# Converting every weight on VectorE, in a new place in the order, and a later cast of the gate, in a fused attention and gated-MLP kernel

## The chip, the core and the metric

The kernel runs on one core of one Trainium2 chip. Its time is the device time of one execution in microseconds (us). A core has five engines with a queue of instructions each: TensorE (PE, with its weight loads shown apart as PEld), VectorE (DVE), ScalarE (ACT), GpSimd (POOL) and SyncE (SP), which here issues all transfers between the large memory and the on-chip memories. Matmuls write to PSUM, a small memory that the kernel uses in three buffers of two banks for most products and in two single banks for the attention's sums.

## The reference

Sigmoid attention over 8 batches, 12 heads, 448 positions and a head size of 64, and behind it a gated MLP with a spatial mix over the positions:

```
scores = q @ k.T / sqrt(64) - log(448)
x      = sigmoid(scores) @ v                   # per batch and head; heads side by side: 448 x 768
h      = max(x @ w_in, 0)                      # 448 x 1024
u, v   = h[:, :512], h[:, 512:]
v_n    = (v - mean(v)) / sqrt(var(v) + 1e-6)   # over the 512 columns
v_s    = w_spatial @ v_n + b_spatial[:, None]
out    = (u * v_s) @ w_out                     # 448 x 768
```

All inputs are 32-bit floats, but w_in and w_out reach the core as 64-bit words, two 32-bit halves an element, which the kernel itself brings into 32-bit floats.

## The kernel before, in words

**Split products.** Outside the attention's second product every operand is held as two parts, hi (the value rounded by a copy into the matmul's 32-bit type) and lo (the value less hi). `split` (lines 99 to 101) makes them: a copy by the engine that it is given, then a subtraction on VectorE. A product takes three matmuls, hi·hi, lo·hi, hi·lo (`TERMS`, line 223).

**Order.** `in_program_order` (lines 18 to 32) ties each engine's instructions to the order in which the program issues them. What stands behind a waiting instruction on its engine waits as well. Waits between engines, and which buffer of a pool a tile gets, are worked out by the tile framework. Python generators interleave the parts: each `next` issues the instructions up to the next `yield`.

**Rounds.** The eight batches go in four rounds m of two (b0 and b1). A round is: attention for both batches, `gate_values` for 7 row tiles in groups of 2, 2, 2, 1 (matmuls pv, 126 of them; relu rv on ScalarE, line 309; statistics and normalization on VectorE and POOL, lines 313 to 337), `spatial` for b0 in two pairs (matmuls pg; addition of the bias on VectorE, line 366), `gated` for b0 in two pairs (matmuls pu; the product g on VectorE, line 388; its split gs, cast on ScalarE and subtraction on VectorE), `spatial` for b1, `output` for b0 in three pairs (matmuls po; copy on ScalarE, line 421; transfer out), `gated` for b1, and `output` for b1. pv, pg, pu, po and the attention's score tiles psc all take their turn in the same three PSUM buffers.

**Attention.** `attention(m)` is a generator: it splits q and k of the first pair of heads, yields, computes three score tiles (psc on TensorE, then a sigmoid at on ScalarE, line 256), yields, and then does the rest. In a round that is not the last, the splits of the next round's attention stand behind `gated(b1, pairs[0])`, the first three score tiles behind `gated(b1, pairs[1])`, and `output` for b1 behind them.

**Weights.** `weight_steps` (lines 140 to 183) is a generator over 22 weights: the first 13 (`NFIRST`, line 186) are six of w_in's second half with the four of w_spatial among them and three of w_in's first half; numbers 13 to 15 are the rest of w_in, 16 to 21 the six blocks of w_out. Each weight first issues the load of the weight two further on (line 159). For a weight below 13, `convert` and the split run on VectorE in three steps. From 13 on (`scalar`), a scaling (line 122) and the copy to hi (line 177) are on ScalarE, VectorE does the rest, and there are four steps. All of it belongs to round 0: attention of round 0 issues 33 steps, one behind most score tiles; the rest are issued by `load_weights(YB)` and its like in lines 490 to 500, ahead of each part of round 0. Two of the 33 steps belong to weight 13.

Of the kernel before, what the change touches and what calls it, by code (L numbers as in the profile page):

```python
# [35 lines left out]
def attn_gmlp_kernel(  # L36
# [67 lines left out]
        return ps_2.tile([P, 2, 512], F32, tag="ps2", name=name)  # L104


    YB = 4

    def convert(l, raw, scalar):

        r = raw.rearrange("p (n w) -> p w n", w=2)
        low, a = r[:, 0], r[:, 1]
        nc.vector.tensor_scalar(l, a, 0x80000000, None, op0=ALU.bitwise_and)


        af = a.bitcast(F32)
        bound = 122879.9921875
        if scalar:

            nc.vector.tensor_scalar(af, af, -bound, bound, op0=ALU.max, op1=ALU.min)  # L120
            yield
            nc.scalar.mul(af, af, 2.0**-112)
        else:
            nc.vector.tensor_scalar(
                a, a, 1, 1, op0=ALU.logical_shift_left, op1=ALU.logical_shift_right
            )
            nc.vector.tensor_scalar(af, af, bound, 2.0**-112, op0=ALU.min, op1=ALU.mult)
        yield
        nc.vector.scalar_tensor_tensor(  # L129
            l, a, 3, l, op0=ALU.logical_shift_left, op1=ALU.bitwise_or  # L130
        )
        nc.vector.scalar_tensor_tensor(  # L132
            l, low, 29, l, op0=ALU.logical_shift_right, op1=ALU.bitwise_or
        )
        yield
# [4 lines left out]
    def weight_steps():  # L140

        steps = []
        for i in range(NCC):
            steps += [(w_in, w_in_s, NCC + i)] + [(w_sp, w_sp_s, i)] * (i < NFC)
        steps += [(w_in, w_in_s, i) for i in range(NCC)]
        steps += [(w_out, w_out_s, i) for i in range(NFC * DM // 512)]
        raws = {}

        def load(n):
            if n < len(steps):  # L150
                src, _, i = steps[n]
                w = 512 if src is w_sp else 1024

                if n < NFIRST:
                    raw = work.tile([P, 1024], U32, tag="tmp", name=f"wraw_{n}", bufs=3)[:, :w]
                else:
                    raw = work.tile([P, 1024], U32, tag="raw", name=f"wraw_{n}", bufs=4)
                raws[n] = raw.bitcast(F32) if src is w_sp else raw
                nc.sync.dma_start(raws[n], src[:, i * w : (i + 1) * w])

        for n in range(AHEAD):
            load(n)
        yield
        for n, (src, dst, i) in enumerate(steps):
            load(n + AHEAD)
            if src is w_sp and i == 0:
                nc.sync.dma_start(b_bc, b_sp.broadcast_to([P, 512]))
            hi, lo = dst[:, i, 0], dst[:, i, 1]
            scalar = n >= NFIRST
            val = raws.pop(n)  # L170
            if src is not w_sp:
                raw = val
                val = work.tile([P, 512], U32, tag="wval", name=f"wval_{n}", bufs=1)
                yield from convert(val, raw, scalar)
                val = val.bitcast(F32)
            if scalar:
                nc.scalar.copy(hi, val)
                yield
            else:
                nc.vector.tensor_copy(hi, val)  # L180
            nc.vector.tensor_sub(lo, val, hi.bitcast(F32))
            if not scalar:
                yield


    NFIRST = NCC + NFC + 3

    weights = weight_steps()

    def load_weights(n):  # L190
        for _ in range(n):
            next(weights, None)
# [152 lines left out]
    def spatial(b, fcs):  # L345

        odd = b % 2
        cols = cols_of(b)
        pg = banks(f"pg_{b}_{fcs[0]}")
        for i, fc in enumerate(fcs):  # L350
            fs = slice(fc * P, (fc + 1) * P)
            pairs = []
            for c in range(NFULL):
                vn = vns[c + 4 if odd else c]
                pairs.append(
                    (lambda a, vn=vn: vn[:, a, fs], lambda p, c=c: w_sp_s[:, c, p, cols])
                )

            short = vns[NFULL][:, odd, fs]
            product(  # L360
                pg[:, i, :S], pairs, [(short, w_sp_s[:, NFULL, a, cols]) for a in range(2)]
            )
        g = work.tile([P, 2, 512], F32, tag="tmp", name=f"g_{b}_{fcs[0]}", bufs=3)[:, :, :S]
        bb = b_bc[:, cols]
        bb = bass.AP(bb.tensor, bb.offset, [list(bb.ap[0]), [0, 2], list(bb.ap[1])])
        nc.vector.tensor_add(g, pg[:, :, :S], bb)
        gates[b, fcs] = g

    hidden = {}

    def gated(b, fcs):

        odd = b % 2
        g = gates.pop((b, fcs))
        pu = banks(f"pu_{b}_{fcs[0]}")
        for i, fc in enumerate(fcs):
            fs = slice(fc * P, (fc + 1) * P)
            product(
                pu[:, i, :S],
                [  # L380
                    (
                        lambda a, cc=cc: w_in_s[:, cc, a, fs],
                        lambda c, cc=cc: x_s[:, c, cc, odd * S : (odd + 1) * S],
                    )
                    for cc in range(NCC)
                ],
            )
        nc.vector.scalar_tensor_tensor(g, pu[:, :, :S], 0.0, g, op0=ALU.max, op1=ALU.mult)  # L388
        gs = work.tile([P, 2, 2 * S], F32R, tag="split", name=f"gs_{b}_{fcs[0]}", bufs=3)
        gs = gs.rearrange("p a (i s) -> p a i s", i=2)  # L390
        split(gs[:, 0], gs[:, 1], g, nc.scalar.copy)
        for i, fc in enumerate(fcs):
            hidden[b, fc] = gs[:, :, i]
# [36 lines left out]
    def start_loads(m):  # L430
        n = m * 2 * NHP
        ahead(attention_loads, n)
        ahead(attention_loads, n + 1)
        ahead(value_loads, n)
        ahead(attention_loads, n + 2)

    def attention(m):

        first, end = 2 * NHP * m, 2 * NHP * (m + 1)
        waiting = []  # L440

        def scores(n, tiles):
            for t in tiles:
                if t == 1:
                    ahead(attention_splits, n + 1)
                if n + 2 < end and t == NFULL + 1:
                    ahead(attention_splits, n + 2)
                waiting.append((*units[n], t, attention_scores(*units[n], t)))
                if n + 2 < end:
                    if t == 0:  # L450
                        ahead(attention_loads, n + 3)
                        ahead(value_loads, n + 2)
                    elif t == NFULL and n + 4 < end:
                        ahead(attention_loads, n + 4)
                if m == 0 and (n > first or t > NFULL) and t != 2:
                    load_weights(1)

        def sums(n):
            for args in waiting[:n]:
                attention_values(*args)  # L460
            del waiting[:n]

        attention_splits(*units[first])
        yield
        for n in range(first, end, 2):
            scores(n, range(NFULL))
            if n == first:
                yield
            scores(n, [NFULL])
            sums(NFULL + (n > first))  # L470
            scores(n, range(NFULL + 1, TILES))
            sums(len(waiting) - NFULL - 1)
        sums(NFULL + 1)
# [13 lines left out]
    for m in range(B // 2):  # L487
        for _ in running:
            pass
        load_weights(YB)  # L490
        for ts in ((0, 1), (2, 3), (4, 5), (6,)):
            load_weights(YB)
            gate_values(m, ts)
        b0, b1 = 2 * m, 2 * m + 1
        for fcs in pairs:
            load_weights(YB)
            spatial(b0, fcs)
        for fcs in pairs:
            load_weights(2 * YB)
            gated(b0, fcs)  # L500
        for fcs in pairs:
            spatial(b1, fcs)
        start_loads(m + 1)
        for es in outs:
            output(b0, es)
        gated(b1, pairs[0])
        last = m == B // 2 - 1
        if not last:
            running = attention(m + 1)
            next(running)  # L510
        gated(b1, pairs[1])
        if not last:
            next(running)
        early = outs if last else outs[:1]
        for part in range(2):
            for es in early:
                output(b1, es, part)
        for es in outs[len(early) :]:
            output(b1, es)
# [53 lines left out]
```

## Time and profile before

| what | us |
|---|---|
| median of 3 runs (lowest, highest) | 702.55 (702.3, 702.74) |
| the profiled execution, its own time | 703.04 |
| its span, first to last instruction | 701.3 |
| TensorE busy | 685.6 (98%) |
| VectorE busy | 285.6 (41%) |
| ScalarE busy | 252.2 (36%) |
| mean granted TensorE clock | 0.994 |

A row of a timeline gives the start in us from the span's start, the length, the engine, the line, the operation, the tile written and those read, the shapes and a count; behind it, in brackets, stands how long the engine had been idle and which instruction ended that. A row of waits gives the engine and tile that waited, what released it, and the total in us, the number of times and the longest. A clock of 1.00 is TensorE's full granted speed.

### The profile page before, as it was taken

The page shows a single profiled execution, that of the slowest core. Times are in us where ns is not written, and L with a number is a line of the kernel's source. Part 1 is how long each engine was busy: PE and PEld are TensorE (multiplying, and loading weights), DVE is VectorE, ACT ScalarE, POOL GpSimd, SP SyncE. Part 2 cuts the span into 40 slices and gives each one's busy share as a digit, 9 for nine tenths or more (in the row PEclk, how much of TensorE's full clock was granted, in tenths as well). Part 3 has the DMA queues.
Part 4 walks back from the last instruction along what each step waited for, and adds up shares of the span by engine and source line. Part 5 has one row for each costly group of instructions (what it writes and reads, how often), then busy time and mean ns, then how long its engine had stood idle before and what let it go on. Part 6 is the DMA issues. An engine that isn't in the chain of part 4 may idle for free.

```text
span 701.3 us, 9100 instructions
## 1 busy us (share of the span) xinstructions
PE 685.6 (98%) x3839; PEld 506.4 (72%) x3839; DVE 285.6 (41%) x451; ACT 252.2 (36%) x302; POOL 18.5 (3%) x36
## 2 busy tenths in 40 slices
PE   9999996999999999999999999999999999999997
PEld 5454885998745468999864548899985455889996
DVE  6997767714124326420414233722122341462110
ACT  6887221212286711001347761101135764101111
POOL 0000001000000001000000000100000000110000
PEclk9999998999999999999999999999999999999999
DMA  8872221212344300003044320000305320000102
GB/s 314 292 251 82 60 61 57 79 59 72 106 157 133 106 1 0 1 1 131 1 158 158 117 68 0 1 1 26 106 27 195 101 73 1 1 1 0 53 27 79
DMA packets 20392, 55.37 MB, mean 79 GB/s; under 512 B 1920, under 2 KB 8192, under 8 KB 20352
## 3 DMA queue, kind: packets, MB, share of 16 engines
q1 hardware_dynamic: 20352, 54.80, 23.1%
q8 instruction: 30, 0.49, 0.3%
q14 instruction: 10, 0.08, 0.0%
HBM read 43.78 MB, written 11.01 MB: 78 GB/s over the span
## 4 chain that ended last, share of the span: by engine, by line
PE 91%; DVE 4%; ACT 2%; issue 1%; POOL 1%; DMA 0%; ACTq 0%; SPq 0%
PE pav L278 19%; PE pu L289 17%; PE po L289 17%; PE psc L248 13%; PE pv L289 12%; PE pg L289 9%; PE psc L236 3%; DVE vn L330 1%; DVE stats L313 1%; ACT rv L309 1%; DVE wval L132 1%; PE idle L482 0%; DVE g L388 0%; DVE wval L129 0%; DVE vn L329 0%
## 5 line engine op out<-in xcount | busy, mean ns | idle before, releaser
L256 ACT ACTIVATE at<-psc,bias_s 128x896 f32<-128x896 f32 x168 | 158.2, 1008 | 42.5 <-PE psc L248 40.1
L278 PE MATMUL pav<-at,v 128*64 128x448 f32 (+1 forms) x768 | 139.4, 546 | 0.0
L289 PE MATMUL pu<-x_s,w_in_s 128*128 128x448 f32 x576 | 120.6, 370 | 5.7 <-ACT rv L309 5.7
L289 PE MATMUL po<-gs,w_out_s 128*128 128x448 f32 x576 | 119.9, 368 | 3.0 <-ACT at L256 3.0
L289 PEld LDWEIGHTS pu<-x_s,w_in_s 128*128 128x128 f32 x576 | 110.0, 191 | 15.2 <-ACT rv L309 6.1
L289 PEld LDWEIGHTS po<-gs,w_out_s 128*128 128x128 f32 x576 | 107.9, 188 | 14.1 <-ACT at L256 4.1
L289 PE MATMUL pv<-w_in_s,x_s 128*128 128x512 f32 x504 | 115.4, 390 | 0.0
L289 PEld LDWEIGHTS pv<-w_in_s,x_s 128*128 128x128 f32 x504 | 94.3, 188 | 22.3 <-issue 2.8
L248 PEld LDWEIGHTS psc<-qks 64*128 64x128 f32 x864 | 77.1, 186 | 39.4 <-ACT at L256 15.5
L278 PEld LDWEIGHTS pav<-at,v 128*64 128x64 f32 (+1 forms) x768 | 44.0, 135 | 82.2 <-issue 75.5
L248 PE MATMUL psc<-qks 64*128 64x448 f32 x864 | 103.0, 378 | 0.2
L101 DVE TENSOR_TENSOR x_s<-pav,x_s 128x448 fp32r<-128x448 f32 x48 | 29.6, 623 | 127.3 <-ACT x_s L100 127.3
L289 PE MATMUL pg<-w_sp_s,vn 128*128 128x448 f32 x352 | 73.2, 365 | 0.8 <-ACT rv L309 0.8
L289 PEld LDWEIGHTS pg<-w_sp_s,vn 128*128 128x128 f32 x352 | 65.9, 187 | 7.0 <-ACT rv L309 1.1
L388 DVE SCALAR_TENSOR_TENSOR g<-pu,g 128x896 f32<-128x896 f32 x16 | 17.5, 1091 | 126.0 <-PE pu L289 126.0
L421 ACT COPY osb<-po 128x896 f32<-128x896 f32 x24 | 21.8, 907 | 119.2 <-PE po L289 108.6
L100 ACT CAST gs<-g 128x896 fp32r<-128x896 f32 x16 | 15.1, 942 | 128.8 <-DVE g L388 128.8
L101 DVE TENSOR_TENSOR qks<-raw,qks 128x832 fp32r<-128x832 f32 (+2 forms) x49 | 49.3, 1007 | 4.7 <-ACT qks L100 3.3
L309 ACT ACTIVATE rv<-pv 128x1024 f32<-128x1024 f32 (+1 forms) x16 | 14.6, 914 | 75.7 <-PE pv L289 75.7
L100 DVE CAST qks<-raw 128x832 fp32r<-128x832 f32 (+1 forms) x39 | 22.6, 578 | 38.5 <-PE po L289 36.4
L313 DVE BATCH_NORM_STATS2 stats<-rv 128x6 f32<-128x512 f32 x28 | 19.0, 679 | 42.9 <-ACT rv L309 42.9
L100 ACT CAST x_s<-pav 128x448 fp32r<-128x448 f32 x48 | 25.5, 532 | 27.8 <-PE pav L278 27.8
(36 smaller groups left out, 231.7 us busy)
## 6 DMA issues: line engine op xcount, KB each, us to landing
raw<-qk_dram SPq DMA_DIRECT2D x47, 448.0 KB, 4.3
v<-v_dram SPq DMA_DIRECT2D x24, 448.0 KB, 4.7
out_dram<-osb SPq DMA_DIRECT2D x24, 448.0 KB, 2.6
wraw<-w_in_dram SPq DMA_DIRECT2D x12, 512.0 KB, 4.1
wraw<-w_out_dram SPq DMA_DIRECT2D x6, 512.0 KB, 3.8
wraw<-w_sp_dram SPq DMA_DIRECT2D x4, 256.0 KB, 5.2
raw<-qk_dram SPq DMA_DIRECT2D x1, 320.0 KB, 3.0
b_bc<-b_sp_dram SPq DMA_DIRECT2D x1, 256.0 KB, 5.8
```

Source lines behind the costliest of these rows:

```text
L100: copy(hi, src)
L101: nc.vector.tensor_sub(lo, src, hi.bitcast(F32))
L132: nc.vector.scalar_tensor_tensor(l, low, 29, l, op0=ALU.logical_shift_right, op1=ALU.bitwise_or)
L236: nc.tensor.matmul(psc[odd * HALF : (odd + 1) * HALF, j, :S], raw[rows, PART : PART + HALF], raw[rows, REST:PART], start=True, stop=True,)
L248: nc.tensor.matmul(psc[:, j, :S], s[rows, a, k : k + P], s[rows, e, REST:PART], start=i == 0, stop=i == len(TERMS) - 1,)
L256: nc.scalar.activation(at, psc[:, :, :S], AF.Sigmoid, bias=bias_s, scale=QK)
L278: nc.tensor.matmul(pav[heads, :S], vt[rows, t, heads], at[rows, j], start=start, stop=stop)
L289: nc.tensor.matmul(ps, st, mv, start=start and i == 0, stop=stop and i == len(ops) - 1)
L309: nc.scalar.activation(rv[:, :n], pv[:, :n], AF.Relu)
L313: nc.vector.bn_stats(stats, rv[:, i])
L388: nc.vector.scalar_tensor_tensor(g, pu[:, :, :S], 0.0, g, op0=ALU.max, op1=ALU.mult)
L421: nc.scalar.copy(osb, po[:, :, :S])
```

## The change

It has two parts. First, the form with ScalarE is gone from `convert` and `weight_steps`: every weight is converted in three steps on VectorE alone, with the two instructions (shift, then bound and scale) that stood only below weight 13, and with the copy to hi on VectorE. The calls that issue the steps move too. Behind round 0's attention stand six steps in one go, before the first normalization; then one step behind each group of `gate_values`; then three steps behind each `spatial` and `gated` of b0 and behind each `spatial` of b1. Before, four steps stood ahead of each part, eight ahead of each `gated`, and none at `spatial` of b1.

Second, `gated` is cut in two: `gated` ends with the product, and `gated_splits` issues the cast and the subtraction. Everywhere but at one place the two stand together. For the second pair of b1, in a round that is not the last, the first score tile of the next round (and its sigmoid) is issued between them. For this `attention` yields behind each of its first three score tiles.

```
-    def convert(l, raw, scalar):
+    def convert(l, raw):
...
-        if scalar:
-
-            nc.vector.tensor_scalar(af, af, -bound, bound, op0=ALU.max, op1=ALU.min)
-            yield
-            nc.scalar.mul(af, af, 2.0**-112)
-        else:
-            nc.vector.tensor_scalar(
-                a, a, 1, 1, op0=ALU.logical_shift_left, op1=ALU.logical_shift_right
-            )
-            nc.vector.tensor_scalar(af, af, bound, 2.0**-112, op0=ALU.min, op1=ALU.mult)
+        nc.vector.tensor_scalar(
+            a, a, 1, 1, op0=ALU.logical_shift_left, op1=ALU.logical_shift_right
+        )
+        nc.vector.tensor_scalar(af, af, bound, 2.0**-112, op0=ALU.min, op1=ALU.mult)
         yield
...
-            if scalar:
-                nc.scalar.copy(hi, val)
-                yield
-            else:
-                nc.vector.tensor_copy(hi, val)
-            nc.vector.tensor_sub(lo, val, hi.bitcast(F32))
-            if not scalar:
-                yield
+            split(hi, lo, val, nc.vector.tensor_copy)
+            yield
...
+    BLOCK = 3
...
         nc.vector.scalar_tensor_tensor(g, pu[:, :, :S], 0.0, g, op0=ALU.max, op1=ALU.mult)
+        products[b, fcs] = g
+
+    def gated_splits(b, fcs):
+
+        g = products.pop((b, fcs))
         gs = work.tile([P, 2, 2 * S], F32R, tag="split", name=f"gs_{b}_{fcs[0]}", bufs=3)
...
-            scores(n, range(NFULL))
-            if n == first:
-                yield
+            for t in range(NFULL):
+                scores(n, [t])
+                if n == first:
+                    yield
...
-        load_weights(YB)
+        load_weights(2 * BLOCK)
         for ts in ((0, 1), (2, 3), (4, 5), (6,)):
-            load_weights(YB)
             gate_values(m, ts)
+            load_weights(1)
         b0, b1 = 2 * m, 2 * m + 1
         for fcs in pairs:
-            load_weights(YB)
             spatial(b0, fcs)
+            load_weights(BLOCK)
         for fcs in pairs:
-            load_weights(2 * YB)
             gated(b0, fcs)
+            gated_splits(b0, fcs)
+            load_weights(BLOCK)
         for fcs in pairs:
             spatial(b1, fcs)
+            load_weights(BLOCK)
...
         gated(b1, pairs[0])
+        gated_splits(b1, pairs[0])
...
         gated(b1, pairs[1])
         if not last:
             next(running)
+        gated_splits(b1, pairs[1])
+        if not last:
+            next(running)
+            next(running)
```

More of the change, by code (lines that the diff above doesn't have):

```diff
@@ L104, in banks @@
         return ps_2.tile([P, 2, 512], F32, tag="ps2", name=name)
-    YB = 4
-    def convert(l, raw, scalar):
+    def convert(l, raw):
         r = raw.rearrange("p (n w) -> p w n", w=2)
@@ L168, in weight_steps @@
             hi, lo = dst[:, i, 0], dst[:, i, 1]
-            scalar = n >= NFIRST
             val = raws.pop(n)
@@ L173, in weight_steps @@
                 val = work.tile([P, 512], U32, tag="wval", name=f"wval_{n}", bufs=1)
-                yield from convert(val, raw, scalar)
+                yield from convert(val, raw)
                 val = val.bitcast(F32)
-            if scalar:
-                nc.scalar.copy(hi, val)
-                yield
-            else:
-                nc.vector.tensor_copy(hi, val)
-            nc.vector.tensor_sub(lo, val, hi.bitcast(F32))
-            if not scalar:
-                yield
+            split(hi, lo, val, nc.vector.tensor_copy)
+            yield
     NFIRST = NCC + NFC + 3
+    BLOCK = 3
     weights = weight_steps()
@@ L369, in attn_gmlp_kernel @@
     hidden = {}
+    products = {}
     def gated(b, fcs):
```

## The prediction

> **What bounds the kernel now.** I read the page first, then TensorE's timeline in order of time with the two stretches as windows, then the waits, and at each gap the timeline of the engine that ended it.
>
> ```profile
> PE 685.6 (98%) x3839; PEld 506.4 (72%) x3839; DVE 285.6 (41%) x451; ACT 252.2 (36%) x302; POOL 18.5 (3%) x36
> ```
>
> TensorE is busy for 685.6 of 701.3 us, so only its 15.7 us of gaps, and time in which it is busy at a low clock, can be won. The work is four rounds of two batches. Round 0 is the only one that converts weights, so round 1 shows what the same matmuls take without that.
>
> ```profile
> 69.71 28.86 PE L289 MATMUL pv<-w_in_s,x_s 128*128 128x512 f32 x126
> 98.41 4.69 PE L289 MATMUL pg<-w_sp_s,vn 128*128 128x448 f32 x22
> 103.87 4.67 PE L289 MATMUL pg<-w_sp_s,vn 128*128 128x448 f32 x22 [0.77 <-ACT rv L309]
> 114.28 17.40 PE L289 MATMUL pu<-x_s,w_in_s 128*128 128x448 f32 x72 [5.74 <-ACT rv L309]
> 131.52 9.24 PE L289 MATMUL pg<-w_sp_s,vn 128*128 128x448 f32 x44
> 140.60 14.95 PE L289 MATMUL po<-gs,w_out_s 128*128 128x448 f32 x72
> ...
> 250.10 28.86 PE L289 MATMUL pv<-w_in_s,x_s 128*128 128x512 f32 x126
> 278.80 9.24 PE L289 MATMUL pg<-w_sp_s,vn 128*128 128x448 f32 x44
> 287.88 14.75 PE L289 MATMUL pu<-x_s,w_in_s 128*128 128x448 f32 x72
> 302.46 8.96 PE L289 MATMUL pg<-w_sp_s,vn 128*128 128x448 f32 x44
> 311.26 14.95 PE L289 MATMUL po<-gs,w_out_s 128*128 128x448 f32 x72
> ```
>
> ```profile
> 69.71:140.60 70.89, 64.39 (x288) 55.53 (x287) 50.17 (x88) 16.57 (x24) 4.58 (x8) 0.95 0.20 64
> 250.10:311.26 61.16, 61.16 (x288) 53.76 (x287) 26.30 (x45) 6.09 (x7) 4.58 (x8) 1.00 0.00 1
> 116.00:118.00 2.00, 2.00 (x7) 1.78 (x6) 1.49 (x3) 0.00 (x0) 0.44 (x1) 0.50 0.00 0
> ```
>
> (In a window row: length, then busy time of PE, PEld, DVE, ACT, POOL, then the granted clock.) The same 288 matmuls from the first pv to the first po take 70.89 us in round 0 and 61.16 us in round 1: **9.73 us** are lost. By start times: pg to pu is 15.87 against 9.08 (6.79 lost, the waits of 0.77 and 5.74 and their restart); pu is 17.24 against 14.58 (2.66 lost; the last window row shows a clock of 0.50 and 7 matmuls in 2 us, where 72 in 14.58 are 9.9); the second pg is 9.08 against 8.80 (0.28 lost, with no wait in the row).
>
> Both waits name the relu (rv, line 309) that empties a PSUM buffer. What held the second relu:
>
> ```profile
> 113.09 0.65 ACT L122 ACTIVATE wraw<-wraw 128x512 f32<-128x512 f32 x1 [1.73 <-DVE wraw L120]
> 113.65 0.58 ACT L309 ACTIVATE rv<-pv 128x512 f32<-128x512 f32 x1
> ```
>
> ScalarE stood at a weight's scaling (line 122), issued ahead of the relu, until VectorE, behind the previous normalization, had done line 120 (the row's 1.73 us of idleness). The pv matmuls were long done (98.41). So ScalarE's order ties the relu to VectorE's lateness.
>
> The other gap is at the end of rounds 0, 1 and 2:
>
> ```profile
> PE po L289 <- ACT at L256: 3.0, 3, 1.0
> ```
>
> ```profile
> 170.06 2.13 PE L248 MATMUL psc<-qks 64*128 64x448 f32 x18
> 171.30 0.94 ACT L100 CAST gs<-g 128x896 fp32r<-128x896 f32 x1 [6.35 <-DVE g L388]
> 172.14 2.80 ACT L256 ACTIVATE at<-psc,bias_s 128x896 f32<-128x896 f32 x3
> 172.27 1.09 DVE L101 TENSOR_TENSOR gs<-g,gs 128x896 fp32r<-128x896 f32 x1 [1.01 <-ACT gs L100]
> 173.20 15.05 PE L289 MATMUL po<-gs,w_out_s 128*128 128x448 f32 x72 [1.01 <-ACT at L256]
> ```
>
> po takes the PSUM buffer of the first score tile, whose sigmoid stands behind the gate's cast.
>
> **The change, part by part.**
>
> *ScalarE* loses lines 122 and 177 for nine weights (steps 13 to 21 of 22): a relu then waits for its matmuls alone. By round 1 it starts 8.50, 16.65 and 24.82 us after the first pv matmul:
>
> ```profile
> 258.60 1.02 ACT L309 ACTIVATE rv<-pv 128x1024 f32<-128x1024 f32 x1 [7.85 <-PE pv L289]
> 266.75 1.02 ACT L309 ACTIVATE rv<-pv 128x1024 f32<-128x1024 f32 x1 [7.13 <-PE pv L289]
> 274.92 1.02 ACT L309 ACTIVATE rv<-pv 128x1024 f32<-128x1024 f32 x1 [7.13 <-PE pv L289]
> ```
>
> *VectorE* gains two instructions a weight. The all-vector form already runs in the trace:
>
> ```profile
> 60.26 0.44 DVE L113 TENSOR_SCALAR wval<-wraw 128x512 uint32<-128x512 uint32 x1
> ...
> 61.69 0.69 DVE L129 SCALAR_TENSOR_TENSOR wval<-wraw,wval 128x512 uint32<-128x512 uint32 x1
> 62.41 0.69 DVE L132 SCALAR_TENSOR_TENSOR wval<-wraw,wval 128x512 uint32<-128x512 uint32 x1
> ...
> 64.09 0.42 DVE L180 CAST w_in_s<-wval 128x512 fp32r<-128x512 f32 x1
> ...
> 65.27 0.43 DVE L113 TENSOR_SCALAR wval<-wraw 128x512 uint32<-128x512 uint32 x1
> ```
>
> From start to start the first step (three instructions) is 1.43, the second (two) 0.72 + 0.72 = 1.44, the third (two) 1.18: **4.05 us a weight**. What stands between the steps comes from these rows:
>
> ```profile
> 70.39 0.62 DVE L101 TENSOR_TENSOR x_s<-pav,x_s 128x448 fp32r<-128x448 f32 x1 [1.79 <-ACT x_s L100]
> 80.74 0.69 DVE L313 BATCH_NORM_STATS2 stats<-rv 128x6 f32<-128x512 f32 x1 [1.64 <-ACT rv L309]
> 86.19 0.68 DVE L129 SCALAR_TENSOR_TENSOR wval<-wraw,wval 128x512 uint32<-128x512 uint32 x1
> 91.59 0.69 DVE L313 BATCH_NORM_STATS2 stats<-rv 128x6 f32<-128x512 f32 x1 [1.69 <-ACT rv L309]
> 98.43 0.69 DVE L129 SCALAR_TENSOR_TENSOR wval<-wraw,wval 128x512 uint32<-128x512 uint32 x1
> 114.26 0.69 DVE L313 BATCH_NORM_STATS2 stats<-rv 128x6 f32<-128x512 f32 x1 [1.25 <-ACT rv L309]
> 117.67 0.68 DVE L129 SCALAR_TENSOR_TENSOR wval<-wraw,wval 128x512 uint32<-128x512 uint32 x1
> ```
>
> A normalization occupies VectorE for 5.45 us (two full tiles), 6.84 (the group with the halved tile) or 3.41 (one tile), POOL's part included. Stats start when the relu has ended, 0.03 later (113.65 + 0.58 to 114.26): 1.05 after the start of a relu of 1.02.
>
> Now the new order by VectorE's clock. The two attention steps of weight 13 add 2.8 us from 65.27 and end near 68.1, ahead of the last x_s subtraction at 70.39, which waits for the last pav; pv keeps its start of 69.71. The six steps ahead of the first normalization then run from 70.94 (the next start after that row's 0.62, less overlap): 13's third step 72.1, weight 14 76.2, two steps of 15 79.0. The first relu starts at 69.71 + 8.50 = 78.2, so stats go at 79.3: nothing late. Normalization to 84.7, one step to 85.9. Stats of the second group at 69.71 + 16.65 + 1.05 = 87.4, to 94.3, one step 95.7; the third is ready at 95.6, runs 95.7 to 101.1, one step 102.6; the fourth to 106.0, one step 107.1. From there gate additions (line 366) and gate products (line 388, with cast and subtraction) alternate with three steps each; I take 1.0 us for an addition and, from 171.30 and 172.27 with a product of 1.1 ahead, 3.1 for a product and its splits: addition 108.1, weight 17 112.2, addition 113.2, weight 18 117.2, product 120.3, weight 19 124.4, product 127.5, weight 20 131.5, addition 132.5, weight 21 136.6, addition 137.6.
>
> TensorE unstalled, at round 1's offsets from 69.71: pg 98.4, pu 107.5, second pg 122.1, po 130.9. What it needs:
> - pu's first buffer, relu of the last pv: ScalarE is idle and empties it by 100. Its second, addition 108.1, needed 114.8.
> - Second pg: product of 117.2 (with 1.1, 118.3), needed 126.5.
> - po: split gate 127.5, needed 131 and later. Weight 20 (block 4 of w_out) serves the first output tile's fourth chunk, nine matmuls of 0.21 (14.95/72) in, at 132.8: **1.3 us spare**. Weight 21 serves the third tile's fourth chunk, 33 matmuls in, at 137.7: **1.1 us spare**.
>
> So all of 6.79 + 2.66 comes back, and of the 0.28 without a cause anything between nothing and all; the first pg of every round has the slow pace too, so I count a quarter: **9.5 us** (bounds 9.4 and 9.7).
>
> The clock: the row has 0.50 right behind the 5.74 us gap, and no dip at the 0.77 or 1.01 us gaps, so 2.66 goes with that gap. The Trainium skill (TensorE: Matmul & The Clock Gate, Part 1: The HAM clock gate) puts the drop at an idle window of about 3.4 us; by that too no drop is left here, and a late weight would cost only its own wait until it is that long. No row here shows the threshold.
>
> The skill also speaks against the direction: Perfetto Trace Analysis, Optimizing Scalar/DVE Operations, advises to offload a saturated VectorE to ScalarE. The window has VectorE at 50.17 of 70.89 us and ScalarE at 16.57, so by that rule the change loads the fuller engine; the sum by it is the rival on the slower side. The trace agrees that VectorE is close to full, not that it sets the end.
>
> *DMA and SP's queue*: the same loads in the same order.
>
> ```profile
> wraw<-w_out_dram SPq DMA_DIRECT2D x6, 512.0 KB, 3.8
> ```
>
> Each load waits for a raw buffer, free when the weight four before it is past its second step, so weight 21's goes by about 111 and lands 3.8 later, for 132.5. The next round's loads queue behind, the third about 130, against a need after 160. Cost nothing; without that cover a load's 3.8.
>
> *The round's end*: 18 matmuls make three score tiles in 2.13, so the first is done about 0.7 to 0.9 after 170.06 and its sigmoid can start near 171.0 and end near 172.0 (2.80 for three with overlap, 1.0 for one); the cast follows at 171.9, its subtraction ends near 174.0. The third score tile still needs the product, and the score matmuls end at 172.19 either way. po starts then at 172.05 to 172.2 instead of 173.20: **1.1 us**, bounds 1.0 and 1.15, in three rounds **3.3**. The subtraction is wanted by po's second half, 12 matmuls (2.5 us) in, at 174.6: 0.6 spare. Behind the cast stand two sigmoids, needed by later po tiles, each 5 us apart; behind the subtraction a split of scores used after po. Nothing is lost there.
>
> Sum: 9.5 + 3.3 = 12.8. The profiled execution takes 703.04 (span 701.3 and 1.74 around it), 0.49 above the median of 702.55; from the former it gives 690.2, from the latter **689.8**, which I forecast.
>
> **The rivals.**
> - *VectorE a little late.* If a weight costs over 0.2 us more than 4.05 (1.1 us over the 5.7 weights in the unbroken run from 95.7 on), po waits for weight 21. With 0.5 more it is 2.85 - 1.1 = 1.75 late: 691.5. For: about 1 us spare at the end of a 66 us run. Against: the price is of the same seven instructions, beside the same engines. 13%.
> - *The swap is worth nothing*, because po waits for the third score tile or the next sigmoid: 689.8 + 3.3 = 693.1. Against: the score matmuls end 1.01 before po starts. 7%.
> - *The clock does not come back*: the 0.50 stretch has another cause and recurs: 689.8 + 2.7 = 692.5. Against: it follows the only long gap. 5%.
> - *Slower: VectorE becomes the bound of round 0.* Place: po of the first batch at weights 20 and 21. It decides where 5.7 weights run 1.1 + 12.8 = 13.9 us longer, from 6.5 us a weight; at 7 us the time is 689.8 + 5.7 x 2.95 - 1.1 = 705.5. For: VectorE would be busy for about 26.30 + 8.7 x 3.8 = 59 of the 68 us to 137.6. Against: 4.05 is measured. 2%.
> - *The change doesn't do what it says*: the order of instructions or buffers comes out so that a relu still waits: about 700 to 702.5. 3%.
>
> **How the numbers follow.** The forecast has 70%, its own range 689.2 to 690.6 (0.28 of pace, 0.3 of the swap, a few tenths of lateness). With the late VectorE and the clock the range is 688.9 to 692.6, which leaves out some 15%. A measurement here tells 0.2% (1.4 us) from no change; every case but the last two is faster by more: faster 95%, same 2%, slower 3%.
>
> **What would show it.** Round 0 from first pv to first po near 61.2 us with clock 1.00 and no wait of pu for rv; stats of round 0 at 79.3 and 87.4; weight 21's last subtraction near 136.6 and no wait of po for VectorE; po at the round's end with no wait for at, the ScalarE order at, gs, at, at. Wrong: any PE wait above 0.3 us between 70 and 146, or a first normalization later than 79.5.

## The result and the profile after

The changed kernel takes 689.73 us (median of 4 runs, 689.42 to 690.46) against 702.42 (4 runs, 701.41 to 702.74): a ratio of 0.9823 with a 95% interval of 0.9806 to 0.984. The forecast was 689.8. The profiled execution takes 689.54 with a span of 687.8, 13.5 less than before.

TensorE's timeline of round 0 of the kernel after, and the windows from the first pv to the first po in rounds 0 and 1 (length, busy time of PE, PEld, DVE, ACT, POOL, clock, share and rate of the transfers); the window from 116 to 118 is the one that had a clock of 0.50 before. The line numbers in the rows are each kernel's own: the matmuls' line 289 is line 275 here.

```profile
69.22 28.86 PE L275 MATMUL pv<-w_in_s,x_s 128*128 128x512 f32 x126
97.91 9.24 PE L275 MATMUL pg<-w_sp_s,vn 128*128 128x448 f32 x44
106.99 14.75 PE L275 MATMUL pu<-x_s,w_in_s 128*128 128x448 f32 x72
121.58 8.96 PE L275 MATMUL pg<-w_sp_s,vn 128*128 128x448 f32 x44
130.38 14.95 PE L275 MATMUL po<-gs,w_out_s 128*128 128x448 f32 x72
```

```profile
69.22:130.38 61.16, 61.16 (x289) 53.78 (x287) 51.91 (x96) 6.11 (x7) 4.58 (x8) 1.00 0.21 66
116.00:118.00 2.00, 2.00 (x12) 1.85 (x11) 1.22 (x2) 0.74 (x1) 0.00 (x0) 1.00 0.72 229
238.77:299.93 61.16, 61.16 (x288) 53.77 (x287) 26.30 (x45) 6.11 (x7) 4.58 (x8) 1.00 0.00 1
```

Round 0 now takes the same 61.16 us as round 1: no row has a wait in brackets, the clock is 1.00, and all of the 9.73 us came back. VectorE is busy for 51.91 of the 61.16 us, and TensorE does not notice.

The end of round 0, on ScalarE and TensorE:

```profile
160.75 1.01 ACT L242 ACTIVATE at<-psc,bias_s 128x896 f32<-128x896 f32 x1 [6.03 <-PE psc L234]
161.66 0.93 ACT L100 CAST gs<-g 128x896 fp32r<-128x896 f32 x1
162.49 1.91 ACT L242 ACTIVATE at<-psc,bias_s 128x896 f32<-128x896 f32 x2
```

```profile
145.16 5.02 PE L275 MATMUL pu<-x_s,w_in_s 128*128 128x448 f32 x24
...
159.84 2.13 PE L234 MATMUL psc<-qks 64*128 64x448 f32 x18
161.89 0.88 PE L275 MATMUL po<-gs,w_out_s 128*128 128x448 f32 x3
```

The order is sigmoid, cast, two sigmoids, and po starts as the score matmuls end. (The first and last PE rows end at the edge of the window that was asked for.) From b1's first pu to its first po it is 16.73 us; before it was 173.20 - 155.39 = 17.81. That is 1.08 a round, 3.24 in three. Together 9.73 + 3.24 = 12.97 of the span's 13.5; the remaining 0.5 is the first pv's start, 69.22 against 69.71, which the change does not touch (last section).

### The profile page after: what moved, and what is told of

The parts are those of the page before. It is cut to its first block, busy times and chain, and to the rows that moved or that the text cites. A ratio compares the mean times of both kernels' runs of the same rounds, so it can differ in the third digit from the quotient of the medians.

```text
span 687.8 us, 9085 instructions
## 1 busy us (share of the span) xinstructions
PE 681.3 (99%) x3839; PEld 503.8 (73%) x3839; DVE 292.8 (43%) x469; ACT 241.3 (35%) x284; POOL 18.5 (3%) x36
## 4 chain that ended last, share of the span: by engine, by line
PE 98%; DMA 1%; SPq 0%; ACT 0%; issue 0%
PE pav L264 20%; PE po L275 17%; PE pu L275 17%; PE pv L275 17%; PE psc L234 14%; PE pg L275 10%; PE psc L222 3%; DMA v<-v_dram 1%; SPq L191 0%; ACT osb L413 0%
## 5 line engine op out<-in xcount | busy, mean ns | idle before, releaser
L275 PE MATMUL pu<-x_s,w_in_s 128*128 128x448 f32 x576 | 118.0, 365 | 0.0
L275 PEld LDWEIGHTS pu<-x_s,w_in_s 128*128 128x128 f32 x576 | 108.2, 188 | 8.5
```

The lines of the kernel that those rows point to most:

```text
L275: nc.tensor.matmul(ps, st, mv, start=start and i == 0, stop=stop and i == len(ops) - 1)
```

## The experiments

Each run is compared with the kernel before on the same chip (702.3 us there, 702.42 beside the kernel after). The kernel after was not run beside them; where a run is set against its 689.73, the two were taken at different times, between which the kernel before agrees to 0.15. Every run computes all that the kernel computes.

**The later cast undone.**

```
         gated(b1, pairs[1])
+        gated_splits(b1, pairs[1])
         if not last:
             next(running)
-        gated_splits(b1, pairs[1])
-        if not last:
             next(running)
             next(running)
```

> The kernel after, with the gate's cast put back ahead of the first score tile's sigmoid; the weights stay as changed. My theory: the two parts add up. The later cast is worth the 1.08 us by which the stretch from b1's first pu to b1's first po got shorter (17.81 to 16.73), three times, 3.2 us: 689.7 + 3.2 = 692.9, with po waiting 1.0 for the sigmoid at three places again. Rival (the swap is worth nothing, the whole gain is round 0): 689.7.

Measured: 693.54 us (693.32 to 693.62), ratio 0.9873 (0.9858 to 0.9887). The wait is back, three times:

```profile
PE po L275 <- ACT at L242: 3.0, 3, 1.0
```

The swap is worth 3.8 between the medians. The profiled executions differ by 3.96: 3.24 of it by the stretch above, and 0.66 is the first pv's start again (69.88 in this profile, 69.22 in the other).

**The later cast alone**, in the kernel before: `gated` and `gated_splits` apart and `attention` yielding behind each of three tiles, the weights as they were.

> The kernel before, with the later cast alone. My theory: 702.4 - 3.2 = 699.2, round 0 as before with its waits of 0.8 and 5.7 us and the clock at half behind them. Rival (the gain came from the weights alone): 702.4. Rival (the two parts need each other): something else than 3.2 between this run and the kernel before, or than the difference to the run without the swap.

Measured: 699.13 us (698.66 to 699.88), ratio 0.9954 (0.9939 to 0.9969), 3.2 below the kernel before. Round 0 keeps its two waits:

```profile
103.83 4.67 PE L289 MATMUL pg<-w_sp_s,vn 128*128 128x448 f32 x22 [0.76 <-ACT rv L309]
114.23 16.84 PE L289 MATMUL pu<-x_s,w_in_s 128*128 128x448 f32 x72 [5.73 <-ACT rv L309]
```

pu is a little less slow than before: it takes 130.91 - 114.23 = 16.68 us here and 17.24 there, 0.56 less, with a gap of the same length ahead of it (last section). From b1's first pu to its first po it is 171.52 - 154.78 = 16.74 us, as in the kernel after; and in the run without the later cast, round 0 takes 131.04 - 69.88 = 61.16, as in the kernel after. So by the stretches the two parts are independent. The medians add up less exactly, 3.2 for the cast alone and 8.8 for the weights alone against 12.7 for both; the first pv's start (up to 1 us) and the slow stretch of pu (0.56 between these two profiles) differ from execution to execution.

**Weights on VectorE, at the old places.** The next two runs part the weights' change into the engine and the places.

```
-        load_weights(2 * BLOCK)
+        load_weights(BLOCK)
         for ts in ((0, 1), (2, 3), (4, 5), (6,)):
+            load_weights(BLOCK)
             gate_values(m, ts)
-            load_weights(1)
...
         for fcs in pairs:
+            load_weights(2 * BLOCK)
             gated(b0, fcs)
             gated_splits(b0, fcs)
-            load_weights(BLOCK)
```

(and likewise around `spatial` of b0, with none at `spatial` of b1.)

> The kernel after, every weight on VectorE in three steps, but the steps issued at the places of the kernel before (one weight ahead of each part, two ahead of each gated of b0). Theory one, ScalarE's order was the cause: no relu stands behind a weight's scaling any more, so the waits of 0.8 and 5.7 us and the half clock go even with the old places; but the addition on the first pg moves behind three more weights, to 117.6 by the prediction's clock, and the second pair's pu, due at 114.8, waits 2.8 us for that buffer: 689.7 + 2.8 = 692.5, clock 1.00. Theory two, the places were the cause: the wait of about 6 us and the half clock stay, 689.7 + 9.5 = 699.2.

Measured: 693.03 us (692.73 to 693.48), ratio 0.9865 (0.9848 to 0.9881). Timelines of TensorE and VectorE, and windows over the stretch to the first po and over the one wait:

```profile
98.96 9.24 PE L275 MATMUL pg<-w_sp_s,vn 128*128 128x448 f32 x44
108.03 7.45 PE L275 MATMUL pu<-x_s,w_in_s 128*128 128x448 f32 x36
117.70 7.69 PE L275 MATMUL pu<-x_s,w_in_s 128*128 128x448 f32 x36 [2.21 <-DVE g L352]
```

```profile
115.95 0.69 DVE L124 SCALAR_TENSOR_TENSOR wval<-wraw,wval 128x512 uint32<-128x512 uint32 x1
116.56 1.08 DVE L352 TENSOR_TENSOR g<-pg,b_bc 128x896 f32<-128x896 f32 x1
117.56 0.42 DVE L100 CAST w_out_s<-wval 128x512 fp32r<-128x512 f32 x1
```

```profile
70.26:134.31 64.05, 61.84 (x289) 53.66 (x287) 56.08 (x103) 6.10 (x7) 4.59 (x8) 1.00 0.21 68
115.50:117.70 2.20, 0.00 (x0) 0.00 (x1) 2.17 (x4) 0.00 (x0) 0.00 (x0) 1.00 0.04 8
```

The waits for the relu and the half clock are gone; the stretch is 64.05 us, 2.9 longer than after. (The medians differ by 3.3; the profiled execution is the slowest of its four, 3.94 above that of the kernel after, and 1.04 of this is a first pv at 70.26.) What is left is the wait that theory one had worked out: the second pu's buffer is emptied by the bias addition (line 352), which stands behind eight more steps than in the kernel after (18 instead of 10 since the attention), nearly three weights. Behind that wait, in the windows from 118 to 126, the clock is 1.00.

**The old conversion with ScalarE, at the new places.** `convert` and the tail of `weight_steps` of the kernel before, four steps a weight, `BLOCK = 4`, all else as after.

> The kernel after with the conversion of the kernel before for weights 13 to 21 (scaling and copy to hi on ScalarE, four steps a weight), issued at the new places: eight steps ahead of the first normalization, one behind each group, four at each later place. Theory one, it takes VectorE: relus wait behind ScalarE's scaling again, at least 5 us lost, 695 or more. Theory two, it takes the places alone: only the first relu stands behind a scaling (79.2 instead of 77.7 us), which later slack swallows; a weight costs VectorE about 4.45 with its waits for ScalarE, so weight 20 is done about 132.8 against a need of 132.4, and the whole costs 0 to 0.8 us: 689.7 to 690.5.

Measured: 689.80 us (689.58 to 690.05), ratio 0.982 (0.9805 to 0.9835): the same as the kernel after. Its ScalarE timeline around the first two relus, and its window:

```profile
78.89 0.66 ACT L120 ACTIVATE wraw<-wraw 128x512 f32<-128x512 f32 x1 [1.68 <-DVE wraw L118]
79.45 1.01 ACT L308 ACTIVATE rv<-pv 128x1024 f32<-128x1024 f32 x1
...
86.12 1.03 ACT L308 ACTIVATE rv<-pv 128x1024 f32<-128x1024 f32 x1 [5.67 <-PE pv L288]
```

```profile
69.47:130.63 61.16, 61.16 (x289) 53.76 (x287) 46.53 (x82) 15.04 (x21) 4.59 (x8) 1.00 0.21 66
```

Theory two holds: the first relu still stands behind a scaling and starts 1.5 us later than it could (10.0 behind the first pv instead of 8.5), the others wait for their matmuls alone, and the stretch is 61.16 again. So **the places alone bring the whole of round 0's gain; the move to VectorE adds nothing to them.** Put at the old places, the move brings all but 2.9 us. Either one undoes the knot, in which relus stood behind ScalarE steps that wait for a busy VectorE; at the new places only the first relu is still held by one, and TensorE loses nothing by it.

**How much room VectorE has.** The sign mask of a weight is issued once more, which changes no value: once in each of weights 16 to 21, then three times.

```
-        nc.vector.tensor_scalar(l, a, 0x80000000, None, op0=ALU.bitwise_and)
+        for _ in range(1 + again):
+            nc.vector.tensor_scalar(l, a, 0x80000000, None, op0=ALU.bitwise_and)
```

> The kernel after, with one instruction repeated (the sign mask, 0.43 us, 0.46 from start to start) in each of the six weights 16 to 21: 2.8 us more for VectorE ahead of the end of weight 21. By the prediction's spare time of 1.1 us po waits 1.7 us: 691.4. By the trace of the kernel after, where weight 21 ends at 135.1 and the matmul that needs its second part stands at about 137.3, the spare is 2.1 to 2.2 us and po waits 0.6: 690.3. Rival, VectorE is far from the bound: 689.7.

> The same instruction repeated three times in each of the weights 16 to 21: 8.3 us more for VectorE. With 2.1 us spare po waits about 4.8 us at weight 20 and 1.3 us at weight 21, 6.1 in all: 695.8 if the clock stays full, up to 698.5 if the gap of 4.8 us drops the clock to 0.50 and costs 2.7 as the gap of 5.7 us did before. With 1.1 us spare: 696.9 or up to 699.6. It is the slower rival's mechanism in a small dose: a loss per weight of 1.4 us beyond the spare.

Measured: once 691.13 us (690.47 to 691.26), three times 696.79 (696.31 to 696.92). The first is read from its profile, since 0.76 of the 1.59 between the profiled executions is the first pv's start (69.98). First the kernel after's weight 21 on VectorE, then TensorE's po in the run with one:

```profile
131.15 0.41 DVE L111 TENSOR_SCALAR wval<-wraw 128x512 uint32<-128x512 uint32 x1
...
134.44 0.69 DVE L101 TENSOR_TENSOR w_out_s<-wval,w_out_s 128x512 fp32r<-128x512 f32 x1
135.05 1.08 DVE L352 TENSOR_TENSOR g<-pg,b_bc 128x896 f32<-128x896 f32 x1
```

```profile
131.14 7.38 PE L276 MATMUL po<-gs,w_out_s 128*128 128x448 f32 x34
138.69 8.06 PE L276 MATMUL po<-gs,w_out_s 128*128 128x448 f32 x38 [0.17 <-DVE w_out_s L101]
```

The 35th matmul starts at 138.69, where an even pace of 0.205 from 131.14 gives 138.11: 0.58 late, waiting for weight 21's second part. From first pv to b1's first pu this run takes 76.62 us, the kernel after 75.94: 0.68 for 2.8 us of added work. The spare is 2.1 us, not the prediction's 1.1. It is no more than that: VectorE is not far from the bound.

The run with three waits where it was said, at weight 20, the tenth matmul of po, and its clock then does something that was not foreseen:

```profile
130.63 2.01 PE L276 MATMUL po<-gs,w_out_s 128*128 128x448 f32 x9
136.71 0.47 PE L276 MATMUL po<-gs,w_out_s 128*128 128x448 f32 x1 [4.07 <-DVE w_out_s L100]
137.44 14.53 PE L276 MATMUL po<-gs,w_out_s 128*128 128x448 f32 x62 [0.26 <-DVE w_out_s L101]
```

```profile
133.00:136.00 3.00, 0.00 (x0) 0.00 (x0) 2.83 (x6) 0.00 (x0) 0.00 (x0) 1.00 0.00 0
137.50:138.00 0.50, 0.50 (x2) 0.46 (x3) 0.50 (x1) 0.00 (x0) 0.00 (x0) 0.85 0.67 229
138.00:138.50 0.50, 0.50 (x3) 0.44 (x2) 0.50 (x2) 0.00 (x0) 0.00 (x0) 0.50 1.02 409
...
141.00:141.50 0.50, 0.50 (x3) 0.48 (x2) 0.47 (x2) 0.00 (x0) 0.00 (x0) 0.73 0.00 0
```

The clock (third column from the end) is full while TensorE idles and through the restart at 136.71, falls at 137.85 (0.85 in a half-us window is 0.15 us at half speed) and is back at 141.27. In the dip about ten matmuls start 0.37 apart instead of 0.205, which costs about 1.5 us and swallows the second wait: weight 21 is done by the time the slowed matmuls reach it. In all the stretch from first pv to b1's first pu is 82.33 - 75.94 = 6.4 us longer, near the expected 6.1 but with other parts: 4.2 of waiting for weight 20's first part, 0.6 for its second and the restart, 1.6 in and right after the dip. The dip can last longer in other executions: the mean clock is 0.997 in the runs of 696.31 and 696.69 us and 0.995 in those of 696.90 and 696.92.

**The cast still later**, behind all three sigmoids.

```
         if not last:
             next(running)
-        gated_splits(b1, pairs[1])
-        if not last:
             next(running)
             next(running)
+        gated_splits(b1, pairs[1])
```

> The kernel after, with the gate's cast behind all three score tiles' sigmoids instead of the first alone. po still starts when the first sigmoid is done, but its second half, 12 matmuls in, wants the subtraction's result, which now comes about 1.9 us later than at 163.7, at 165.6, against a need of 164.9: a wait of about 0.7 us at three places, 691.7. Rival, only the first sigmoid's place matters: 689.7.

Measured: 692.56 us (692.07 to 692.99), 2.8 more than the kernel after, 0.9 a round (0.8 by the stretch from po to the next score tile). TensorE waits in the middle of po, as expected:

```profile
161.87 3.23 PE L275 MATMUL po<-gs,w_out_s 128*128 128x448 f32 x14
165.54 12.17 PE L275 MATMUL po<-gs,w_out_s 128*128 128x448 f32 x58 [0.45 <-DVE gs L101]
```

Twelve matmuls of po's first half and two of its second run, then the third of the second half needs the subtraction's result. So of the three places tried, the one between the first sigmoid and the second is the best: ahead of the first the cast costs a round 1.08, behind the third 0.8 to 0.9. Behind the second was not tried.

**The end of the kernel**, which the change leaves: the last output copied and sent in two halves.

```
+        if b == B - 1 and es == outs[-1]:
+            for i, e in enumerate(es):
+                nc.scalar.copy(osb[:, i], po[:, i, :S])
+                nc.sync.dma_start(out[b, e], osb[:, i])
+            return
```

> The kernel after, with the very last output copied and sent in two halves, one for each of its two output tiles. The end of the kernel is not part of the change: the trace has 0.91 us of copy behind the last matmul and a transfer behind that. The first half's copy should run under the second half's matmuls, so the last copy falls to about 0.5 us and its transfer to half the bytes: 0.4 to 0.9 us less, 688.8 to 689.3. Rival, the transfer's fixed time rules or a second transfer costs as much: 689.7 or a little more.

Measured: 689.91 us (689.25 to 690.39, 5 runs), no difference to 689.73.

```profile
683.60 0.97 ACT L415 COPY osb<-po 128x448 f32<-128x448 f32 x2 [1.50 <-PE po L275]
```

Both halves start behind the last matmul, one after the other: 0.97 instead of 0.91. The first half was not released early, so its copy hid under nothing, and two transfers of half the size won nothing either. What holds the first half was not looked into.

## Why the prediction was right, point by point

- **The bound and the size of the loss in round 0** were right: 9.73 us between rounds, and 9.73 came back. I had counted 9.5, a quarter of the 0.28 us by which the second pg was slow; all of it returned (130.38 - 121.58 = 8.80). Its cause stays open; it is not the clock, since the run with the weights at the old places has the slow 9.08 (125.23 to 134.31) at a full clock.
- **Its cause** was right in kind: the relu stood behind a scaling that waited for VectorE. But the prediction let ScalarE's relief and the new places appear as one. The runs show two cures: the places alone 689.80, the engine alone 693.03, both 689.73. The prediction had the trace agree that VectorE is close to full; 50.17 of 70.89 us is 71%, so that was too strong. What the Trainium skill (Perfetto Trace Analysis, Optimizing Scalar/DVE Operations) says of a saturated VectorE, that offloading some work to ScalarE may make sense, costs nothing here and gains nothing: at the new places ScalarE's form frees VectorE by 51.91 - 46.53 = 5.4 us that nobody waits for.
- **VectorE's clock** was right in its order and close in its times: first stats at 78.77 (forecast 79.3), second at 86.93 (87.4), weight 20 done at 130.23 (131.5), weight 21 at 135.13 (136.6). 0.5 of each difference is the earlier first pv. The rest is the one mis-sized term: 4.05 us a weight. Followed by an addition a weight takes 131.15 to 135.05, 3.90, mostly because the next instruction starts 0.61 after the subtraction, not 0.73 as in the pair of rows that I had. Over the 5.7 weights that is 0.85 us; with the second part wanted one matmul, 0.2 us, later than I had counted, the spare time is 2.1 instead of 1.1, as the run with one repetition shows (0.68 lost, where 1.1 of spare would have lost 1.7).
- **The rival of a late VectorE** is thus a real mechanism, further off than I put it, and at three repetitions it is there with its price.
- **The clock** came back with the gap, as forecast. The waits of 0.77, 1.0 and 2.2 us show no dip, those of 4.1 and 5.7 do.
- **The round's end**: 3.3 forecast, 3.24 by the stretch, 3.2 between the medians of the kernel before and of the cast alone. The subtraction's spare was put too low: its result is first used by the third matmul of po's second half, at about 164.9 in the kernel after, 1.2 us behind its end at 163.7, where I had counted 0.6 to the first; so 1.9 us later cost 0.8 to 0.9 a round and not 1.3.
- **The sum**: 12.8 forecast, 12.97 in the stretches, 12.7 between the medians. That the time came out within 0.1 us of the forecast is luck in part. I read the loss in round 0 from one execution: it is 9.73 there and 140.00 - 69.67 - 61.16 = 9.17 in the run with the cast alone, whose round 0 has the same instructions; and the first pv's start differs by up to 1 us between executions.
- **The chances**: "same 2%, slower 3%" does not follow from the rivals, which give 2% to a slower kernel and 3% to one that hardly changes. Nothing hangs on it.

## What to carry to other kernels

Do not let the instruction that empties a PSUM buffer stand in a queue behind one that waits for a backlogged engine; moving the background work behind the critical instruction cured it here at least as well as moving it to another engine (689.80 against 693.03 us), so try the order first. Give background work in small steps behind each critical step, sized by where its result is next needed, and place a cast behind the step that is waited for first, but no later than its own result is wanted. And read the lost time off a twin stage (here round 1) before summing single waits: the twin also holds the slow clock and the slow pace that no row of waits names.

## What was not expected of the hardware

- **The clock can fall after the work has resumed.** With 4.07 us of waiting, TensorE restarted at 136.71 at full speed and was halved only at 137.85, for 3.4 us. In the kernel before, the dip began within the gap of 5.74 us and lasted twice as long:

```profile
112.50:113.00 0.50, 0.00 (x0) 0.00 (x0) 0.47 (x2) 0.00 (x0) 0.00 (x0) 0.54 0.83 287
...
119.00:119.50 0.50, 0.50 (x3) 0.46 (x2) 0.08 (x1) 0.39 (x1) 0.00 (x0) 0.63 0.00 0
```

  that is from 112.54 to 119.37, 6.8 us. In the run with the later cast alone the gap is as long, 5.73 us, and so is the dip, but it lies 0.76 us earlier, from 111.78 to 118.61:

```profile
111.00:112.00 1.00, 0.00 (x0) 0.00 (x0) 0.65 (x1) 0.32 (x1) 0.00 (x0) 0.89 0.34 37
...
114.00:119.00 5.00, 4.77 (x14) 4.27 (x15) 3.87 (x7) 0.18 (x1) 1.10 (x2) 0.54 0.00 0
```

  More of that dip falls into the gap, and pu loses 16.68 - 14.58 = 2.10 us there and 2.66 before. So the price of a gap depends on more than its length: about 1.5 us behind 4.1, and 2.1 or 2.7 behind 5.7.

  What it depends on as well can be read from the clock records that the traces keep, of which the clock column is the mean. The first record of full clock begins at 6.73 us before, at 5.97 with the cast alone and at 4.73 with three repetitions. From there to the fall it is 105.81 us in the first two and 133.12 in the third, 31 and 39 times 3.413 us; and the dips are two, two and one of these 3.413 us long. The fall behind the last matmul lies on the same grid in all ten traces, 200 to 203 times 3.413 us behind the first record. So the clock changes at steps of 3.413 us whose place differs from execution to execution and does not depend on the gap, and where they fall in the gap sets the price. The Trainium skill (TensorE: Matmul & The Clock Gate, Part 1: The HAM clock gate) has free-running windows of about 3.4 us; these traces agree. The Trainium skill puts the drop, in the same section, behind an idle window of that length. By the grid, the window that ended with the fall at 137.85 began at 134.44, and TensorE worked again from 136.71, so that window was not idle throughout. How much of a window must be idle no run here shows.

- **The first pv starts at 69.2 to 70.3 us** over the profiles of these ten kernels, though all issue the same work before it save for the last weight steps. The profiles differ already in the first score tiles (the fourth tile's first matmul starts at 7.73 before and at 6.89 after). The 18 matmuls of the first three score tiles take 2.22 us in the kernel after and 3.46 in the run with the old places, and the first clock record begins at 4.64 and at 7.70 us there; these are the earliest and the latest record, and the latest is that of the latest pv. So much of the spread goes with the time at which TensorE first gets its full clock, though not all: the earliest pv, 69.19 with the cast still later, has a first record at 5.64. (The clock column reads 1.00 where no record stands.) Up to 1 us of a difference between two runs here is that and no effect of an edit, which is why small effects above are read from stretches.
